# Eight input loads of a period: four pairs at neighbouring steps, or a step for each load, and a fourth result buffer

## The chip, the core and the metric

The kernel runs on one core of a Trainium2 chip. The metric is the time of one execution on the device in microseconds (us). The core has five engines that each work through a list of their own in order: TensorE (PE, matmuls, with the weight loads shown as PEld), VectorE (DVE), ScalarE (ACT), GpSimd (POOL) and SyncE (SP). Sixteen DMA engines move data; in this kernel SP issues the transfers of one queue and POOL those of another.

## The reference, cut to what matters

```python
# x: 8 x 3008 x 256, filt_r and filt_i: 1505 x 256
X = np.fft.rfft(x, axis=1)
y = np.fft.irfft(X * (filt_r + 1j * filt_i), n=3008, axis=1)
h = y.reshape(24064, 256) @ moe_w_in                     # 256 -> 2048
g = np.maximum(h, 0.0) + moe_alpha * np.minimum(h, 0.0)
out = g @ moe_w_out                                      # 2048 -> 256
```

## The kernel before, in words

The work has two halves that run side by side. The Fourier half takes one batch (3008 rows) at a time through four stages of small matmuls: piece_a (first DFT, reads a tile `xs` of x), piece_b (second DFT and product with the filter), piece_c (inverse of the second), piece_d (inverse of the first, written to `yT`). Between the stages the data goes out to device memory and comes back turned: `a_dram` between piece_a and piece_b, `v_dram` between piece_c and piece_d (`load_z`, L266). The product with a complex filter needs an exchange of the two halves of the partitions: after DVE has made `uu` and `ww`, POOL issues two adding transfers `uu<-ww` (L236), and piece_c reads `uu`.

The second half is the pair of dense layers, in 48 blocks of 512 (or 384) rows. A block has 16 steps; step s = 16n + j belongs to block n. In each step `up(j)` puts two matmuls of the first layer on PE (L495); after each second step ACT evicts (L503) and DVE applies the slope (L506, L507). The second layer of a block runs 16 steps behind, interleaved with the next block. In 21 of the blocks (`FAST`: 8, 10, 12 up to 42 by twos, then 43 to 45) it is done with seven products in place of eight, by `seven()`, whose 112 matmuls are on L554. Those need sums of quarters of the block, made by `sums()` at the steps of `SUMS`: DVE makes `ss`, and POOL issues adding transfers, one for each half h: `gtb<-gtb` (L519, at steps 16n+10 and 16n+17, read by the sixth product, matmuls 81 to 96) and `gtb<-ss` (L521, at 16n+20 and 16n+21, read by the seventh, matmuls 97 to 112). Below, "the first half" and "the second half" of a block's `gtb<-ss` are these two.

All the Fourier pieces are put into this stream by hand: `put(step, fn)` files a call under a step, and the loop over steps issues what stands there, so the list of steps is the order in which each engine gets its instructions. Nothing waits for the step itself: an instruction whose data is ready runs as soon as its engine has come to it. Batch b has its origin at p = 96(b-1), six blocks a batch; from batch 4 on all batches use the same lists of steps (STEPS_A, STEPS_B and so on), shifted by 96.

The loads of x are what the change touches. A batch's x comes in four tiles `xs` (index c), each filled by two transfers from POOL (L168, one a half of the partitions, 188 KB in float16, cast on the way from float32). There are four `xs` buffers, so the load of (b+1, c) must wait until piece_a of (b, c) has read its tile; piece_a of batch b stands at p-84 to p-43, and that of batch b+1 at p+12 to p+53. For batches 4 to 7 (b = 3 to 6) the pairs of loads stand at p-8, p-4, p and p+4:

```python
put(STEPS_X[b - 1][c] if b < 3 else p - 8 + 4 * c,
    lambda b=b, c=c: xc.update({(b + 1, c): load_x(b + 1, c)}))
```

The results go out through tiles `osb` (pool `p_osb`, three buffers): ACT or DVE fills one (L537, L565 to L572, L474), SP stores it (L464), and a buffer is free again once its stores have landed.

## Time and profile before

| what | value |
|---|---|
| median of 3 runs | 785.37 us (785.03, 785.37, 786.56) |
| the profiled execution | 783.02 us, of which the span is 780.6 us |
| PE busy | 759.1 us (97% of the span) |
| DVE, ACT, POOL busy | 687.2, 605.3, 277.3 us |
| granted TensorE clock | 1.000 |
| `uu<-ww` on POOL (L236) | 168 transfers of 64 KB, 3.2 us from issue to landing (median) |
| `gtb<-gtb` (L519), `gtb<-ss` (L521) | 42 each of 256 KB, 4.2 and 6.1 us |
| `xs<-in_x_dram` (L168) | 64 of 188 KB, 7.0 us |

The profile is of one execution. A line of the groups names the source line, the engine, what is written and what is read; "idle before" is the time that the engine stood still in front of such instructions, with what ended it. "DMA share" in a table of stretches is the mean busy share of the sixteen DMA engines; transfers that begin near its end make it read a little over 1. Spans on POOL are rough: its transfer instructions overlap, and what counts there is when one starts and when its data has landed.

### The profile page before, as it was taken

How to read it: one execution, taken by the hardware profiler on the slowest of the kernel's cores; microseconds unless marked ns; L12 is line 12 of the kernel's file. 1: busy time of each engine (PE TensorE's matmuls, PEld its weight loads, DVE VectorE, ACT ScalarE, POOL GpSimd, SP SyncE). 2: the span in 40 equal slices, each digit the busy share in tenths (PEclk: the TensorE clock that was granted, in tenths of full speed). 3: DMA queues.
4: the chain of work that ended last, by engine and by line, in shares of the span. 5: the costliest groups of instructions: out<-in, count | busy, mean ns of one | idle time of the engine just before them, and what ended most of it. 6: DMA issues, size and time to landing. Idle time of an engine off the chain costs nothing. (4 is left out here: it accounts for less than half of the span.)

```text
span 780.6 us, 18307 instructions
## 1 busy us (share of the span) xinstructions
PE 759.1 (97%) x6952; PEld 540.0 (69%) x6952; DVE 687.2 (88%) x1501; ACT 605.3 (78%) x902; POOL 277.3 (36%) x367
## 2 busy tenths in 40 slices
PE   7899999999999999999999999999999999999998
PEld 6756667666667767676676766767667777777666
DVE  3788996899999899899898989889899999889994
ACT  3787778788778887788877887788878777787763
POOL 7830651245244351553334423434323434102210
PEclk9999999999999999999999999999999999999999
DMA  9996868667988679975888769886797555735642
GB/s 185 193 198 177 154 123 208 177 135 148 202 193 175 148 145 194 236 148 125 169 213 176 138 135 200 188 173 129 160 201 175 112 113 95 180 84 112 121 96 68
DMA packets 115184, 122.93 MB, mean 157 GB/s; under 512 B 12873, under 2 KB 94553, under 8 KB 115097
## 3 DMA queue, kind: packets, MB, share of 16 engines
q0 software_dynamic: 34960, 52.19, 41.0%
q1 hardware_dynamic: 79992, 69.52, 33.4%
q8 instruction: 54, 0.88, 0.5%
q14 instruction: 34, 0.27, 0.1%
q10 hardware_dynamic: 144, 0.07, 0.0%
HBM read 56.06 MB, written 46.66 MB: 132 GB/s over the span
## 5 line engine op out<-in xcount | busy, mean ns | idle before, releaser
L503 ACT ACTIVATE gtb<-hps 128x1024 f16<-128x1024 f32 (+1 forms) x384 | 386.4, 1006 | 106.9 <-PE hps L495 104.3
L495 PE MATMUL hps<-yT,win_s 128*128 128x512 f16 (+1 forms) x1536 | 449.3, 375 | 0.0
L506 DVE TENSOR_SCALAR m<-gtb,alm_s 128x512 f16<-128x512 f16 (+1 forms) x768 | 235.1, 348 | 52.3 <-ACT gtb L503 50.2
L507 DVE TENSOR_TENSOR gtb<-gtb,m 128x1024 f16<-128x1024 f16 (+1 forms) x384 | 261.5, 681 | 17.2
L532 PE MATMUL op<-wout_s,gtb 128*128 128x256 f16 x1600 | 243.3, 272 | 0.0
L532 PEld LDWEIGHTS <-gtb 128*128 128x128 f16 x1600 | 156.0, 98 | 105.1
L236 POOL DMA_DIRECT2D uu<-ww x168 | 141.7, 1041 | 242.7 <-DVE uu L234 131.2
L495 PEld LDWEIGHTS <-win_s 128*128 128x128 f16 x1536 | 136.6, 98 | 25.7 <-issue 2.6
L554 PEld LDWEIGHTS <-gtb 128*128 128x128 f16 x1680 | 114.4, 98 | 57.4 <-DMA gtb<-ss 5.0
L519 POOL DMA_DIRECT2D gtb<-gtb x42 | 41.5, 987 | 197.8 <-DVE ss L515 75.5
L554 PE MATMUL op<-wout_s,gtb 128*128 128x128 f16 x1008 | 85.8, 219 | 4.1 <-DMA gtb<-ss 3.6
L280 ACT ACTIVATE asb<-psF 96x512 f16<-96x512 f32 x112 | 65.4, 595 | 11.5 <-PE psF L210 10.8
L280 ACT ACTIVATE yT<-psF 128x376 f16<-128x376 f32 x120 | 57.3, 490 | 11.0 <-PE psF L273 10.4
L554 PEld LDWEIGHTS <-ss 128*128 128x128 f16 x672 | 47.1, 98 | 23.3
L554 PE MATMUL op<-tw_s,gtb 128*128 128x128 f16 x672 | 58.2, 219 | 0.1
L554 PE MATMUL op<-tw_s,ss 128*128 128x128 f16 x672 | 58.0, 219 | 0.0
L233 DVE TENSOR_TENSOR ww<-psF,filts_s 128x512 f16<-128x512 f32 x84 | 57.4, 683 | 0.0
L234 DVE TENSOR_TENSOR uu<-psF,filt_s 128x512 f16<-128x512 f32 x84 | 57.1, 679 | 0.0
L280 ACT ACTIVATE v<-psF 128x512 f16<-128x512 f32 x84 | 49.9, 599 | 9.1 <-PE psF L248 8.3
L168 POOL DMA_DIRECT2D xs<-in_x_dram x64 | 43.2, 1054 | 20.9 <-PE psF L210 13.5
L521 POOL DMA_DIRECT2D gtb<-ss x42 | 45.7, 1290 | 3.2 <-PE op L554 0.9
L210 PE MATMUL psF<-xs,wf_s 94*96 94x512 f16 x112 | 41.2, 381 | 1.8 <-DVE yT L283 0.5
(85 smaller groups left out, 518.2 us busy)
## 6 DMA issues: line engine op xcount, KB each, us to landing
out_dram<-osb SPq DMA_DIRECT2D x127, 128.0 KB
xs<-in_x_dram POOLq DMA_DIRECT2D x64, 188.0 KB, 7.0
a_dram<-asb SPq DMA_DIRECT2D x28, 384.0 KB
uu<-ww POOLq DMA_DIRECT2D x168, 64.0 KB, 3.2
v_dram<-v SPq DMA_DIRECT2D x112, 96.0 KB
zt<-v_dram SPq DMA_DIRECT2D x28, 384.0 KB
gtb<-gtb POOLq DMA_DIRECT2D x42, 256.0 KB, 4.2
gtb<-ss POOLq DMA_DIRECT2D x42, 256.0 KB, 6.1
```

Of the source, the lines that this page charges most:

```text
L168: nc.gpsimd.dma_start(out=xs[h * N1 : h * N1 + N1], in_=xrow(b, h, c))
L233: nc.vector.tensor_mul(ww, px, filts_s[:, 2 * kp : 2 * kp + 2])
L234: nc.vector.tensor_mul(uu, px, filt_s[:, 2 * kp : 2 * kp + 2])
L236: nc.gpsimd.dma_start(out=uu[o : o + 64], in_=ww[64 - o : 128 - o], accum_op=OP.add)
L280: nc.scalar.activation(o, i, AF.Copy)
L495: nc.tensor.matmul(self.hps[:, j % 2, 0:tn], win_s[:, kt, j * 128 : (j + 1) * 128], yT[:, kt, self.t0 : self.t0 + tn], start=(kt == 0), st ...
L503: nc.scalar.activation(g, hs, AF.Copy)
L506: nc.vector.tensor_scalar(ms[:, i], g[:, i], 0.0, a, OP.min, OP.mult)
L507: nc.vector.tensor_add(g, g, ms)
L521: nc.gpsimd.dma_start(out=a12, in_=z2, accum_op=OP.add)
L532: nc.tensor.matmul(op[:, si % 2], self.pair(k // 2)[:, k % 2, 128 * si : 128 * si + 128], wout_s[:, k], start=(k == 0), stop=(k == 15))
L554: nc.tensor.matmul(acc[:, 128 * i : 128 * i + 128], x[:, k, 128 * i : 128 * i + 128], b[:, k], start=first and k + i == 0, stop=k == 7, sk ...
```

## The change

Each of the eight loads for batches 4 to 7 gets a step of its own, from a new list; the pair that belongs to tile c is at places 2c and 2c+1. The loads of batches 0 to 3 stay where they were. `p_osb` gets a fourth buffer, and the small tile `al16`, used once at the start, is taken from that pool in place of a place of its own.

```diff
+STEPS_Q = (-28, -18, -8, -3, 1, 9, 15, 23)
...
-    p_osb = ctx.enter_context(tc.tile_pool(name="p_osb", bufs=3))
+    p_osb = ctx.enter_context(tc.tile_pool(name="p_osb", bufs=4))
...
-    al16 = konst.tile([16, 128], FP32, name="al16")
+    al16 = p_osb.tile([128, 2, D], FP32, name="osb")[0:16, 0, 0:128]
...
-    def load_x(b, c):
-        xs = p_x.tile([2 * N1, 8 * D], FP16, name="xs")
-        for h in range(2):
-            nc.gpsimd.dma_start(out=xs[h * N1 : h * N1 + N1], in_=xrow(b, h, c))
-        return xs
+    def load_x(b, c, halves=(0, 1)):
+        if 0 in halves:
+            xc[(b, c)] = p_x.tile([2 * N1, 8 * D], FP16, name="xs")
+        for h in halves:
+            nc.gpsimd.dma_start(out=xc[(b, c)][h * N1 : h * N1 + N1], in_=xrow(b, h, c))
...
             for c in range(4):
-                put(STEPS_X[b - 1][c] if b < 3 else p - 8 + 4 * c,
-                    lambda b=b, c=c: xc.update({(b + 1, c): load_x(b + 1, c)}))
+                if b < 3:
+                    put(STEPS_X[b - 1][c], load_x, b + 1, c)
+                else:
+                    for h in range(2):
+                        put(p + STEPS_Q[2 * c + h], load_x, b + 1, c, (h,))
```

On PE, DVE, ACT and SP the order of instructions is the same before and after. On POOL it moves only the 32 loads of batches 4 to 7. With the block that begins at p-32 called the first of a period (n = 10, 16, 22 and 28), POOL's list there changes from the first row to the second:

```
before: uu x4 | L519, uu x2, L519, uu x2, L521 x2, xs x8      | uu x4, L519, uu x2, L519, L521 x2, uu x10
after:  uu x4, xs | L519, uu x2, xs, L519, uu x2, L521 x2, xs x3 | uu x4, xs, L519, uu x2, xs, L519, L521 x2, uu x2, xs, uu x8
```

(So it stands for n = 22 and 28. At n = 16 two `uu` stand in front of the first load instead of four; n = 10 has no `uu` between its transfers, since batch 3 has steps of its own.)

More of the change, by code (lines that the diff above doesn't have):

```diff
@@ L356 @@
     nc.sync.dma_start(out=wfx_s, in_=wfx_d.ap())
-    xc = {(0, c): load_x(0, c) for c in range(4)}
+    xc = {}
+    for c in range(4):
+        load_x(0, c)
     f0 = First()
@@ L434 @@
     for c in range(4):
-        xc[(1, c)] = load_x(1, c)
+        load_x(1, c)
     for q in range(2):
```

## The prediction

> **What bounds the kernel now.** I read the page first, then the waits of PE, then POOL's instructions in order of time around those waits, then the DMA share by stretches.

> ```profile
> PE 759.1 (97%) x6952; PEld 540.0 (69%) x6952; DVE 687.2 (88%) x1501; ACT 605.3 (78%) x902; POOL 277.3 (36%) x367
> ```

> PE is the bound, and the clock is 1.00 throughout. The change takes no matmul away and leaves PE's order alone, so it can only add or remove time in which PE stands still. The waits of PE and of its weight loads from 190 us on (the fast blocks begin there) say how much there is; columns are total us, times, longest:

> ```profile
> PE op L554 <- DMA gtb<-ss: 3.6, 5, 1.2
> PE psF L248 <- DMA uu<-ww: 1.1, 2, 0.9
> ...
> PEld L554 <- DMA gtb<-ss: 5.0, 6, 1.4
> PEld L248 <- DMA uu<-ww: 1.6, 2, 1.1
> ```

> A weight load and its matmul wait together, so the larger figure counts: 5.0 us for `gtb<-ss`, 1.6 for `uu<-ww`. By L521's own rows in narrow windows, three of these waits fall into n = 16 (0.9 us at 320.5), n = 22 (1.4 at 415.3) and n = 28 (1.0 at 509.1): 3.3 us in the blocks whose loads of x are moved. Those are the blocks where the eight loads stand right behind `gtb<-ss`; n = 34 has the same place in its period and no loads, since there is no batch 8. POOL in n = 28, then in n = 34 (start, us, what, idle before):

> ```profile
> 500.18 0.98 POOL L519 DMA_DIRECT2D gtb<-gtb  x1 [3.52 <-DVE ss L515]
> 501.38 1.66 POOL L236 DMA_DIRECT2D uu<-ww  x2 [0.22 <-issue]
> 502.44 2.54 POOL L521 DMA_DIRECT2D gtb<-ss  x2
> 503.62 5.27 POOL L168 DMA_DIRECT2D xs<-in_x_dram  x7
> ```

> ```profile
> 590.64 1.01 POOL L519 DMA_DIRECT2D gtb<-gtb  x1 [3.52 <-PE op L554]
> 591.85 1.66 POOL L236 DMA_DIRECT2D uu<-ww  x2 [0.19 <-PE hps L495]
> 593.87 1.77 POOL L521 DMA_DIRECT2D gtb<-ss  x2 [0.37 <-PE op L554]
> ```

> and L521's two transfers from issue to landing in n = 28, then in n = 34:

> ```profile
> DMA to landing us min/median/max: 4.5/5.8/7.0
> ```

> ```profile
> DMA to landing us min/median/max: 4.1/4.6/5.0
> ```

> n = 34 makes it in time, with 1.8 us to spare (landing 599.49, first read 601.31); n = 28 does not. That gap of 2.0 us in the second half's landing is what the change aims at, whatever its cause. The DMA engines around it (last columns: clock, DMA share, GB/s):

> ```profile
> 397.00:401.00 4.00, 4.00 (x30) 2.77 (x29) 3.90 (x10) 2.44 (x3) 2.34 (x3) 1.00 0.62 119
> 401.00:405.00 4.00, 4.00 (x42) 2.81 (x40) 3.82 (x8) 3.04 (x4) 0.21 (x1) 1.00 0.98 222
> 405.00:409.00 4.00, 4.00 (x52) 3.00 (x50) 3.93 (x10) 2.95 (x6) 3.16 (x6) 1.00 1.07 291
> ...
> 497.00:501.00 4.00, 4.00 (x50) 3.26 (x49) 3.86 (x9) 2.53 (x5) 0.82 (x1) 1.00 1.05 267
> 501.00:505.00 4.00, 4.00 (x59) 3.37 (x57) 3.90 (x12) 3.24 (x7) 3.78 (x8) 1.00 0.97 202
> ```

> They are full from about 401 and 497 us, well before `gtb<-ss` is issued (407.5 and 502.4): the three `zt` loads of SP and the stores of results run there.

> **The change, part by part.**

> *What a load costs where it stands.* On POOL a load takes about 0.53 us of issue (seven begin within 3.6 us). On the DMA engines, in the cluster with nothing of POOL's between, seven loads landed from 511.56 to 517.64 us: 6.08/6 = 1.01 us of all sixteen engines each, if they are full.

> *Two loads move ahead of the first block's transfers.* Nothing waits for a step, so the load of p-28 runs as soon as POOL has issued the `uu` before it; POOL then stands idle for 12.5 to 13.0 us until L519 of the first half. Cost nothing: that idle time hides it, and the half it precedes has 9.7 to 11.1 us to spare. The load of p-18 is issued right behind the next pair of `uu` (about 308.7, 400.6 and 496.1 us) and before L519 of the second half, which waits 3.8, 4.6 and 3.5 us for DVE and PE: no delay on POOL. On the DMA engines it is another matter. It begins to move about 2.3 us after issue (so the first of the cluster at 227.75 did), which is 311, 403 and 498 us, when the engines are full or about to be, and everything behind it in POOL's queue comes later by up to 1.01 us: L519 of the second half, then `gtb<-ss`, on which PE already waits. What the load finds free shortens that: by packet records about half an engine share at 310, 0.2 at 402 to 406, and 0.3 at 503 to 504. So the delay lies between 0.4 and 1.0 us at n = 16, 0.8 and 1.0 at n = 22, 0.7 and 1.0 at n = 28. I take 0.7, 0.9 and 0.8: **+2.4 us**. At n = 10 the same load is issued near 212 us, and the engines have free time until 219: nothing.

> *Five fewer loads behind `gtb<-ss`.* Three still follow at once (p-8, p-3, p+1), because POOL does not wait for their steps. Behind in a queue that is served in order they should cost the transfer ahead nothing; the 2.0 us between n = 28 and n = 34 say otherwise. But n = 34 also issued its `gtb<-ss` 1.0 us later behind its L519 (3.2 against 2.3), so fewer transfers stood in front. I count nothing for the five, since three loads are enough to fill the engines for the 3 us in question. The bound on the other side is the whole of the three waits, -3.3 us.

> [...]

> *Loads in the second block of a period* (n = 12, 18, 24, 30): p+9 ahead of the first half's L519 (11 to 13 us to spare), p+15 ahead of the second's, p+23 behind `gtb<-ss`. The second half of `gtb<-ss` lands 1.45, 2.80, 2.08 and 2.90 us before it is read. One load ahead takes 1.01: no wait. If the one behind cost the 2.0 us above too, n = 12, 24, 18 and 30 would lose 1.6, 0.9, 0.2 and 0.1: between 0 and +2.8; I take 0, as for the five.

> *`uu<-ww`.* The wait of 1.6 us near 486 us comes from `uu` issued at 477 to 478 that took about 8.9 us, beside SP's turn of `a_dram`. The load of p-28 comes right behind these. Between -1.6 (timing shifts) and +1; I take 0.

> *Arrival of x.* Tile 0 gains: it now lands 8.3 to 10.2 us before piece_a and comes 8 to 11 us earlier. The last load comes 20 to 25 us later, out of 34 to 39 us to spare. No wait; tiles 1 and 2 have 25 to 33 us and move by less. The buffers' readers (piece_a up to p-43) are done before p-28.

> *Fourth result buffer.* The three buffers were nearly short where the DMA engines are full: ACT stood 0.4 us before the result of n = 28 (L568) for a store to land, and PE did not wait there. A fourth removes that and would cover stores made later by the loads. On the path: nothing. `al16` is read once before the first result; nothing.

> **Sum.** +2.4 us. The profiled execution took 783.02 us (span 780.6 and 2.4 around it); it would take 785.4, a span of 783.0. The median of the runs stands 2.35 above that execution, so the forecast is 785.37 + 2.4 = **787.8 us**.

> **Rivals.**

> *Faster: the number of loads behind counts.* For it: n = 34. If the three waits vanish, 785.37 - 3.3 = 782.1 us; if the 2.0 us shrink with the number from eight to three, each block gains 1.25 and loses 0.8, 785.37 - 3 x 0.45 = 784.0. It decides from the point where the loads behind cost more than the load ahead. Against: L519 and `gtb<-ss` were already queued into full engines, and three loads follow as closely as before. Chance 0.33, most of it below 783.8.

> *No change: the load ahead is paid by others.* If the engines alternate between POOL's and SP's queues, the load of p-18 takes its time from the stores of results, which nobody waits for with four buffers. Then `gtb<-ss` lands as it did: 785.4 us. Chance 0.2.

> *Slower still: the second blocks wait too.* The +2.8 above on top of +2.4: 790.6 us. For it: only 1.45 and 2.08 us to spare at n = 12 and 24. Chance 0.08, within slower.

> *The change does not do what it says:* for three of the eight loads it does not, since a step is only a place in POOL's list; this is in the forecast already.

> **Numbers.** About 0.2% (1.6 us) is what a measurement of this kernel can tell from no change. Slower (above 786.9): 0.39 for the forecast and 0.08 for the last rival, 0.47 together. Same: 0.20. Faster (below 783.8): 0.33. The slower cases' own range is 787.0 to 790.6. Both signs hold much of the chance, so the range reaches from the faster rival's end, 782.0, to 789.8, just short of the slower rival's.

> **What would show it.** Right: in the profile after, L521's longest landing at 9.5 us in n = 22 (8.7 now) and 7.7 in n = 28 (7.0 now), and PEld's wait for `gtb<-ss` from 190 us at 7 us or more, in the same three blocks. Wrong: that wait at 2 us or less (the number of loads counted), or unchanged with the stores later. A new wait of L554 at n = 12 or 24 would be the last rival; one of piece_a (L210) for `xs` would refute the margins.

## The result, and the profile after

The changed kernel took 790.99 us (median of 8 runs, 785.44 to 792.95), the kernel before 784.81 us in the same comparison (8 runs, 781.39 to 786.93). The ratio is 1.0077, with a 95% interval of 1.0051 to 1.0103: slower by some 6 us. The side was forecast; the size was not (787.8 us, range 782.0 to 789.8). The profiled execution took 790.13 us with a span of 788.3 us, 7.7 us more than the span before.

The page after, first line of the busy times:

```profile
PE 760.2 (96%) x6952; PEld 540.5 (69%) x6952; DVE 687.5 (87%) x1501; ACT 605.3 (77%) x902; POOL 278.3 (35%) x367
```

The same matmuls, 1.1 us more of busy time, and the rest of the 7.7 us of span is PE standing still. The waits of PE and of its weight loads from 190 us on (total us, times, longest); all lines are three further down than before, so L524 is `gtb<-ss`, L522 `gtb<-gtb`, L557 the products, L274 piece_d, L249 piece_c, L170 the loads of x:

```profile
PE op L557 <- DMA gtb<-ss: 4.4, 5, 1.6
PE psF L274 <- DMA zt<-v_dram: 2.3, 1, 2.3
PE psF L249 <- DMA uu<-ww: 1.8, 1, 1.8
PE op L557 <- DMA gtb<-gtb: 1.4, 1, 1.4
...
PEld L557 <- DMA gtb<-ss: 5.3, 5, 1.8
PEld L274 <- DMA zt<-v_dram: 2.4, 1, 2.4
PEld L249 <- DMA uu<-ww: 2.0, 1, 2.0
PEld L557 <- DMA gtb<-gtb: 1.6, 1, 1.6
```

The wait on `gtb<-ss` hardly grew (5.0 us before). What is new is that piece_d waits 2.4 us for `zt`, once (at 319.5 us, in n = 16), that the sixth product waits 1.6 us for `gtb<-gtb` (n = 10), and that `uu<-ww` grew by 0.4. Together these lines give 11.3 us; `gtb<-ss`, `uu<-ww` and `gtb<-gtb` gave 6.9 before.

PE's order is the same, so the two traces can be set side by side matmul by matmul: the time that PE stood still between matmuls at each place, and by how much the matmuls behind the place then run later than before.

| place | stood still before, us | after, us | later by, us |
|---|---|---|---|
| up to 190 us | 9.2 | 11.0 | 1.1 |
| n = 10 | 0.9 | 2.0 | 1.2 |
| n = 16 | 1.2 | 2.7 | 3.2, of which 1.6 are lost at half clock |
| n = 22 | 1.2 | 2.2 | 1.2 |
| `uu<-ww` near 486 to 492 | 1.1 | 1.8 | 0.5 |
| n = 28 | 0.8 | 1.6 | 0.7 |
| n = 43 | 0.5 | 0.2 | -0.2 |

The first row and the last lie outside the moved loads; in the second profile of the same kernel the first 190 us are 0.1 us shorter than before, so the first row is not the change's. That profile (span 784.0 us) also divides the loss otherwise: of the places of the moved loads, n = 22 gains 1.4 us there and n = 28 loses 2.0. So one profile is weak evidence for one place, and several are compared below. The two measures of the table differ by up to 0.7 us (first row).

The half clock is in the table of stretches (last columns: granted clock, DMA share, GB/s):

```profile
316.00:319.50 3.50, 3.50 (x47) 2.85 (x45) 3.40 (x11) 2.81 (x6) 3.28 (x7) 1.00 0.81 134
319.50:322.90 3.40, 1.15 (x19) 0.84 (x16) 2.37 (x7) 0.79 (x3) 2.24 (x4) 1.00 0.99 262
322.90:326.30 3.40, 3.40 (x29) 2.71 (x27) 1.11 (x3) 2.45 (x5) 0.00 (x0) 0.50 1.10 238
326.30:330.00 3.70, 3.24 (x42) 2.41 (x40) 2.23 (x6) 2.46 (x6) 0.00 (x0) 1.00 1.06 223
```

PE is busy for 1.15 of 3.40 us, and in the next 3.41 us it is granted half its clock. A stretch of instructions there took 4.23 us; in a second profile of the same kernel, where the clock stayed at 1.00, it took 2.61. So the wait of 2.4 us cost 4.0 here.

POOL in n = 28 after (start, us, what, idle before), and the times from issue to landing of its two `gtb<-ss` there, then of those of n = 22 and n = 16:

```profile
502.10 1.65 POOL L237 DMA_DIRECT2D uu<-ww  x2 [1.56 <-PE hps L498]
503.18 1.12 POOL L170 DMA_DIRECT2D xs<-in_x_dram  x1
507.29 0.98 POOL L522 DMA_DIRECT2D gtb<-gtb  x1 [2.99 <-DVE ss L518]
508.49 1.65 POOL L237 DMA_DIRECT2D uu<-ww  x2 [0.22 <-issue]
509.55 2.51 POOL L524 DMA_DIRECT2D gtb<-ss  x2
510.73 2.90 POOL L170 DMA_DIRECT2D xs<-in_x_dram  x3
```

```profile
DMA to landing us min/median/max: 5.5/6.6/7.8
...
DMA to landing us min/median/max: 7.0/8.2/9.3
...
DMA to landing us min/median/max: 9.0/9.6/10.1
```

The second half now lands 7.8 us after issue at n = 28 (7.0 before), 9.3 at n = 22 (8.7) and 10.1 at n = 16 (6.7). At n = 16 the matmuls that read it came later still, since piece_d in front of them waited for `zt`.

Where `zt` was lost is on SP. Its list from the last eight stores of results before n = 16 to the loads of `zt`, before and then after:

```profile
298.23 6.99 SPq L464 DMA_DIRECT2D out_dram<-osb  x8
305.27 2.86 SPq L257 DMA_DIRECT2D v_dram<-v  x4
310.29 1.25 SPq L266 DMA_DIRECT2D zt<-v_dram  x3
```

```profile
301.29 8.97 SPq L467 DMA_DIRECT2D out_dram<-osb  x8
310.32 2.33 SPq L258 DMA_DIRECT2D v_dram<-v  x4
316.80 1.52 SPq L267 DMA_DIRECT2D zt<-v_dram  x3
```

and what SP's queue waited for there (from 294 us in both), before and then after:

```profile
SPq L266 <- DMA v_dram<-v: 2.0, 1, 2.0
SPq L464 <- DMA at<-a_dram: 1.1, 2, 0.9
```

```profile
SPq L267 <- DMA v_dram<-v: 4.0, 1, 4.0
SPq L467 <- DMA at<-a_dram: 2.8, 2, 1.6
```

In both traces SP's 479 transfers name eight semaphores in turn: 470 of the last 471 name the one that the transfer eight places before named, and 429 wait for the one that they name. Among the stores of results are those that follow an `at<-a_dram` by eight places. In front of the store eight places behind the last `at<-a_dram`, SP went on at 301.51 us before and 306.27 after, 0.02 and 0.01 us after the last signal that this `at<-a_dram` had landed. Behind these stores in SP's order stand those of `v_dram`, for which `zt` waits (the 2.0 and 4.0 us above). The load of p-28, issued at 293.72 us right behind `uu<-ww`, lands 10.8 us later, so it is in the DMA engines at the same time as the `at<-a_dram` of 291.56 us and later; the last of these four took 8.9 us from issue to landing before and 11.7 after. From the first `at<-a_dram` of the turn to the first load of `zt` it took 20.8 us before and 25.2 after. Some 3.0 us of that are lost up to the last four stores of `v_dram`, and 1.5 behind them, where SP waits 4.0 us in place of 2.0 for these stores; the load of p-18, issued at 310.98 us, stands beside them.

### The profile page after: what moved, and what is told of

Its sections match the earlier page's. It is cut to its first block, busy times and chain, and to the rows that moved or that the text cites. A ratio compares the mean times of both kernels' runs of the same rounds, so it can differ in the third digit from the quotient of the medians.

```text
span 788.3 us, 18315 instructions
## 1 busy us (share of the span) xinstructions
PE 760.2 (96%) x6952; PEld 540.5 (69%) x6952; DVE 687.5 (87%) x1501; ACT 605.3 (77%) x902; POOL 278.3 (35%) x367
## 4 chain that ended last, share of the span: by engine, by line
PE 77%; DMA 9%; DVE 7%; issue 3%; ACT 2%; POOL 2%; SPq 0%; DVEq 0%; POOLq 0%; ACTq 0%
PE hps L498 34%; PE op L535 19%; PE op L557 13%; DMA gtb<-ss 3%; PE psF L211 3%; PE psF L274 2%; PE psF L249 2%; PE psF L231 2%; DVE m L509 2%; DMA uu<-ww 2%; DVE gtb L510 2%; DMA zt<-v_dram 1%; ACT gtb L506 1%; DMA twf_s<-c_twf 1%; DVE ww L234 1%
## 5 line engine op out<-in xcount | busy, mean ns | idle before, releaser
L510 DVE TENSOR_TENSOR gtb<-gtb,m 128x1024 f16<-128x1024 f16 (+1 forms) x384 | 261.6, 681 | 17.2
L557 PEld LDWEIGHTS <-gtb 128*128 128x128 f16 x1680 | 115.0, 98 | 59.7 <-DMA gtb<-ss 5.3
L522 POOL DMA_DIRECT2D gtb<-gtb x42 | 43.0, 1024 | 187.4 <-DVE ss L518 72.1
L557 PE MATMUL op<-wout_s,gtb 128*128 128x128 f16 x1008 | 85.8, 219 | 4.9 <-DMA gtb<-ss 4.4
L281 ACT ACTIVATE asb<-psF 96x512 f16<-96x512 f32 x112 | 65.4, 595 | 11.5 <-PE psF L211 11.3
L557 PEld LDWEIGHTS <-ss 128*128 128x128 f16 x672 | 47.2, 98 | 23.5 <-issue 0.3
L170 POOL DMA_DIRECT2D xs<-in_x_dram x64 | 56.6, 1054 | 15.9 <-PE psF L211 14.2
L557 PE MATMUL op<-tw_s,gtb 128*128 128x128 f16 x672 | 58.9, 221 | 1.4 <-DMA gtb<-gtb 1.4
L557 PE MATMUL op<-tw_s,ss 128*128 128x128 f16 x672 | 58.2, 219 | 0.0
L524 POOL DMA_DIRECT2D gtb<-ss x42 | 45.0, 1252 | 3.2 <-PE op L557 1.0
L274 PE MATMUL psF<-wi_s,zt 96*128 96x94 f16 x504 | 39.8, 206 | 4.3 <-DMA zt<-v_dram 2.9
```

Of the source, the lines that this page charges most:

```text
L170: nc.gpsimd.dma_start(out=xc[(b, c)][h * N1 : h * N1 + N1], in_=xrow(b, h, c))
L274: nc.tensor.matmul(ps[:, m], self.zt[g][:, 4 * mh + m, dh * 128 : dh * 128 + 128], wi3_s, start=True, stop=True)
L281: nc.scalar.activation(o, i, AF.Copy)
L510: nc.vector.tensor_add(g, g, ms)
L557: nc.tensor.matmul(acc[:, 128 * i : 128 * i + 128], x[:, k, 128 * i : 128 * i + 128], b[:, k], start=first and k + i == 0, stop=k == 7, sk ...
```

## The experiments

The theory is that the two loads put ahead of the transfers cost the time: the one of p-18 as forecast, the one of p-28 by way of SP. The rivals are that the loads left behind `gtb<-ss` matter (fewer is faster, or the second blocks of a period suffer), and that the fourth buffer does something. The edits of `STEPS_Q` are to the changed kernel, in the order tile 0 to 3, two halves each. Ratios are to the kernel before run beside them, 5 rounds each, with the 95% interval.

**One part alone: four buffers.** The kernel before, with the fourth buffer and its `al16` only.

```diff
-    p_osb = ctx.enter_context(tc.tile_pool(name="p_osb", bufs=3))
+    p_osb = ctx.enter_context(tc.tile_pool(name="p_osb", bufs=4))
```

> The kernel before with the fourth result buffer alone (and the alpha tile taken from that pool); the loads of x stay in pairs at p-8 to p+4. Theory A (the moved loads cost the time): ratio to before 1.000, within 0.998 to 1.002. Rival B (a fourth buffer lets stores run later and crowds the transfers of the next blocks): 1.003 or more, and the waits of piece_d for zt and of the fast blocks for gtb<-ss grow as in the changed kernel.

Measured: 0.998 (0.9954 to 1.0005), 782.86 us.

**One part undone: three buffers, the loads moved.**

```diff
-    p_osb = ctx.enter_context(tc.tile_pool(name="p_osb", bufs=4))
+    p_osb = ctx.enter_context(tc.tile_pool(name="p_osb", bufs=3))
```

> The changed kernel with three result buffers: the new steps alone. Theory A: 1.006 to 1.010, like the whole change. If the fourth buffer hid stores that the loads make late, more than the whole change, 1.009 to 1.013, with waits of ACT for out_dram<-osb. Rival B: 1.002 or less.

Measured: 1.0104 (1.0065 to 1.0142), 790.59 us. Here PE had waits for an eviction by ACT that the changed kernel lacks, 1.5 us near 415 and 1.1 us near 510 us: ACT itself stood 2.0 and 1.6 us in front of a result buffer whose stores had not landed. So the moved loads make the stores late as well, and the fourth buffer hides that. It is worth something near 2 us beside the moved loads, with an interval that includes nothing.

**One load ahead, or none.**

```diff
-STEPS_Q = (-28, -18, -8, -3, 1, 9, 15, 23)
+STEPS_Q = (-28, -8, -8, -3, 1, 9, 15, 23)
```

> The changed kernel with the load of p-18 put back to p-8: of the two loads ahead of the first block's transfers only that of p-28 is left, and four follow gtb<-ss. Theory A1 (the load of p-28 falls on SP's turn of a_dram; SP's list slips, and the zt loads come 2 to 6 us late): most of the loss stays, 1.004 to 1.008, with the zt loads of n = 16 issued 3 us or more later than before. Theory A2 (the forecast's step: the load of p-18 stands in the queue ahead of gtb<-ss): 1.000 to 1.002.

```diff
+STEPS_Q = (-18, -8, -8, -3, 1, 9, 15, 23)
```

> The changed kernel with the load of p-28 moved to p-18 and that of p-18 to p-8: one load stands ahead of L522's second half, none behind the uu of p-42 and p-41. Theory A1: 1.000 to 1.003, with the zt loads of n = 16 issued at the same step as before (273). Theory A2: most of the loss stays, 1.003 to 1.006, with the gtb<-ss waits of n = 16, 22 and 28 at 5 us together.

```diff
+STEPS_Q = (-8, -8, -8, -3, 1, 9, 15, 23)
```

> The changed kernel with both early loads put back: tile 0's two loads at p-8, so five loads follow gtb<-ss in the first block of a period and the other three stay at p+9, p+15 and p+23. If the two early loads are the whole loss (theory A), 0.997 to 1.000, as the fourth buffer alone (0.998). If the loads at p+9 to p+23, in the second block, cost something of their own (rival C), 1.002 or more, with a wait of the seventh product for gtb<-ss at n = 12, 18, 24 or 30 of 1 us or more.

Measured: p-28 alone 1.0025 (1.0005 to 1.0046), 786.78 us; p-18 alone 1.0015 (0.9993 to 1.0037), 785.94 us; none ahead 0.9991 (0.9965 to 1.0018), 783.5 us. Without the early loads the loss is gone, with five loads behind `gtb<-ss` in place of eight and three spread over the second blocks. PE's weight loads wait there as they did before:

```profile
PEld L557 <- DMA gtb<-ss: 5.2, 7, 1.1
PEld L249 <- DMA uu<-ww: 1.4, 2, 1.2
```

SP's list with p-28 alone, same place as above:

```profile
300.90 7.87 SPq L467 DMA_DIRECT2D out_dram<-osb  x8
308.83 2.10 SPq L258 DMA_DIRECT2D v_dram<-v  x4
313.78 2.30 SPq L267 DMA_DIRECT2D zt<-v_dram  x3
```

The time from the turn's first `at<-a_dram` to the first `zt` before n = 16, 22 and 28, in the profiles of all kernels that have eight loads a batch, three or more behind `gtb<-ss` and none at p-43:

| kernels | n = 16, us | n = 22 | n = 28 |
|---|---|---|---|
| no load at p-28: before, four buffers, none ahead, p-18 alone (two profiles), two at p-18 | 20.8 to 21.8 | 15.3 to 17.2 | 16.7 to 17.1 |
| one load at p-28: changed (two profiles), p-28 alone, three buffers | 23.3 to 25.2 | 17.6 to 19.5 | 17.8 to 18.0 |
| two loads at p-28 | 23.9 | 19.7 | 20.9 |

At all three places every kernel with the load is above every kernel without it, by 0.4 us at the least. The transfers of the turn themselves tell the same: the last of the four `at<-a_dram` takes 8.9 to 9.5, 7.9 to 8.4 and 9.0 to 9.4 us to land in the kernels of the first row, and 10.4 to 11.7, 9.1 to 10.0 and 10.2 to 10.4 us in those of the second. The load at p-18 alone does not move SP.

**Two loads at one place.** Both early loads at p-18, then both at p-28.

```diff
+STEPS_Q = (-18, -18, -8, -3, 1, 9, 15, 23)
```

> The changed kernel with both loads of tile 0 at p-18, none at p-28; three behind gtb<-ss as in the changed kernel. Theory A2 (what counts is the number of bytes ahead of gtb<-ss in POOL's queue): L522's second half and gtb<-ss of n = 16, 22 and 28 come another 1 us later than with one load there: 1.006 to 1.010. Theory A3 (it takes both places together: the load of p-28 delays SP's list, so that its zt loads meet the load of p-18): 1.002 to 1.005.

```diff
+STEPS_Q = (-28, -28, -8, -3, 1, 9, 15, 23)
```

> The changed kernel with both loads of tile 0 at p-28, none at p-18; three behind gtb<-ss as in the changed kernel. Theory A2: nothing ahead of gtb<-ss that has not long landed: 0.998 to 1.001. Theory A1 (SP's list is what slips): 1.005 to 1.010, with the zt loads of n = 16 issued 5 us or more later than before and piece_d waiting for them. Theory A3: 1.002 to 1.005.

Measured: two at p-18 1.0099 (1.0064 to 1.0134), 792.12 us; two at p-28 1.0056 (1.0033 to 1.0078), 788.76 us. Two directly ahead of `gtb<-gtb` and `gtb<-ss` are the dearer pair, by 0.0043, just clear of the two intervals.

**Loads behind.** None behind and two at p-28; none behind and none close ahead (two at p-43 instead); six behind with the same two at p-43.

```diff
+STEPS_Q = (-28, -28, 8, 8, 22, 22, 24, 24)
```

> The changed kernel with tile 0's two loads at p-28 and the other six at p+8 (two), p+22 (two) and p+24 (two): no load follows gtb<-ss in the first block, two run ahead, none at p-18. Rival D (loads behind gtb<-ss slow it, so taking all of them away gains): gtb<-ss lands 4 to 5.5 us after issue at n = 16, 22 and 28, and the ratio is 0.993 to 0.998. Theory A1 (loads behind SP's turn of a_dram make the zt loads late): zt loads of n = 16 are issued 3 us or more late, gtb<-ss lands no sooner than before, 1.002 to 1.008.

```diff
+STEPS_Q = (-43, -43, 7, 7, 23, 26, 28, 33)
```

> The changed kernel with the loads laid around the first block of a period: tile 0's two at p-43, behind gtb<-ss of the block before and ahead of SP's turn of a_dram (p-39); tile 1's two at p+7, tiles 2 and 3 at p+23, p+26, p+28 and p+33. None stands ahead of or behind gtb<-ss at n = 16, 22 and 28. Rival D (the loads behind slow gtb<-ss): it lands 4 to 5.5 us after issue there, as at n = 34, the three waits vanish, and the ratio is 0.994 to 0.998. Theory A (only loads ahead of it cost): it lands as in the kernel with none ahead (6.9 to 8.2 us for the second half), 0.998 to 1.002. If the loads at p-43 still meet SP's turn, the zt loads of n = 16 are issued late again and the ratio is 1.002 or more.

```diff
+STEPS_Q = (-43, -43, -4, -4, 0, 0, 4, 4)
```

> The changed kernel with tile 0's two loads at p-43 and the other six in pairs at p-4, p and p+4, all six behind gtb<-ss of the first block, as in the kernel before with eight. Rival D: gtb<-ss lands 1 to 2.5 us later at n = 22 and 28 than in the kernel with none behind, and the ratio is 0.002 to 0.004 higher than there. Theory A: it lands the same within 0.5 us, and the two ratios agree within 0.002.

Measured: 1.0183 (1.0146 to 1.022), 800.7 us (five runs; a sixth took 811.2 us); 1.0114 (1.0081 to 1.0148), 793.09 us; 1.0137 (1.0108 to 1.0166), 795.36 us. In the first, PE's weight loads wait 9.7 us for `uu<-ww`, in five places (1.6 us before, 3.4 at the most elsewhere). The last two differ only in where the other six loads stand. Their times from issue to landing of `gtb<-ss` at n = 16, with none behind and then with six:

```profile
DMA to landing us min/median/max: 8.8/9.2/9.6
```

```profile
DMA to landing us min/median/max: 8.6/9.0/9.3
```

At n = 22 the second half landed after 8.0 us (none) and 6.7 (six), at n = 28 after 7.9 and 9.1. Loads behind don't slow it in any regular way, and with none behind it is about as slow as in the changed kernel (9.6, 8.0 and 7.9 us against 10.1, 9.3 and 7.8). So the rival finds no support here; both kernels carry the loads at p-43, so it was not tried by itself. The loads at p-43 meet the turn as well: from `at<-a_dram` to `zt` it takes 24.0 us with none behind, 23.1 with six.

**The changed kernel again**, and then its two early loads cut to an eighth in turn. An eighth is the first of the eight rows that each partition takes; the other seven eighths stand at p-8.

> The changed kernel once more, on the chip of the others of this call: 1.005 to 1.010 under every theory. It is the reference for the kernel with the cut load, and a second look at where its waits fall.

```diff
+                        if c == h == 0:
+                            put(p - 28, load_x, b + 1, c, (h,), 0, D)
+                            put(p - 8, load_x, b + 1, c, (h,), D, 8 * D)
```

> The changed kernel with the load of p-28 cut in two transfers: one eighth of its columns at p-28, the other seven eighths at p-8; the load of p-18 stays. If it is the bytes at p-28 that cost (A1), as the kernel with the load of p-18 alone: 1.000 to 1.003. If any transfer in that place does (its turn in POOL's list, its semaphore), as the whole change: 1.006 to 1.010.

Measured: again 1.0069 (1.0045 to 1.0093), 789.38 us, which is the 1.0077 of before; with an eighth at p-28 1.0062 (1.0035 to 1.0088), 788.87 us. The second was to come down to the time of p-18 alone and did not, though SP was back (21.7 us from `at<-a_dram` to `zt`). Either any transfer at p-28 costs, whatever its bytes, or the time of p-18 alone is higher than it seemed. Four kernels on one chip:

> The kernel with the load of p-18 alone ahead (the other at p-8), once more, beside the three kernels that follow. Two theories of what an early load costs. Bytes: the early load costs by the 188 KB that it puts in front of SP's turns and of gtb<-ss. Place: any transfer of POOL at that place costs, however small, because the later transfers of POOL move up by one. Both expect here what this kernel gave before, a ratio of 1.0015 (1.000 to 1.0035), about 786 us.

```diff
+STEPS_Q = (-8, -8, -8, -3, 1, 9, 15, 23)
+                        if c == h == 0:
+                            put(p - 28, load_x, b + 1, c, (h,), 0, D)
+                            put(p - 8, load_x, b + 1, c, (h,), D, 8 * D)
```

> No load ahead but one eighth of a load at p-28 (one eighth of tile 0's first half, its other seven eighths at p-8, where the second half stands too). Bytes: as with none ahead, a ratio of 0.999 (0.997 to 1.0015), 783.5 us, zt loads of n = 16 at step 272 to 273. Place: 1.003 or more, since the same small transfer beside the load of p-18 went with 1.0062.

```diff
+                        if c == 0 and h == 1:
+                            put(p - 18, load_x, b + 1, c, (h,), 0, D)
+                            put(p - 8, load_x, b + 1, c, (h,), D, 8 * D)
```

> The changed kernel with the load of p-18 cut to one eighth there, the other seven eighths at p-8; the load of p-28 stays whole. Bytes: what the load of p-28 alone gave, a ratio of 1.0025 (1.0005 to 1.0045), 787 us, with the second half of gtb<-ss landing 1 us sooner than in the changed kernel at n = 16 (9 instead of 10.1 us from issue). Place: as the changed kernel, 1.007 (1.005 to 1.009), 790 us.

> One eighth of a load at p-28 and the whole load at p-18, once more, now beside the load of p-18 alone on the same chip. Bytes: the two agree within 0.002, near 1.0015, and the 1.0062 of before was a difference between chips. Place: 1.006 again, at least 0.003 above the load of p-18 alone.

Measured: p-18 alone 1.0002 (0.9982 to 1.0022), 784.72 us; the eighth at p-28 alone 1.0027 (1.0005 to 1.0049), 786.79 us; p-28 whole and an eighth at p-18 1.009 (1.0058 to 1.0121), 790.81 us; an eighth at p-28 and p-18 whole 1.0063 (1.004 to 1.0085), 788.87 us. So it looked as if the place costs, whatever the bytes. But all these kernels have nine transfers a batch where the others have eight. Two more put the ninth elsewhere:

```diff
+STEPS_Q = (-18, -8, -8, -3, 1, 9, 15, 23)
+                        if c == 0 and h == 1:
+                            put(p - 8, load_x, b + 1, c, (h,), 0, D)
+                            put(p - 8, load_x, b + 1, c, (h,), D, 8 * D)
```

> The load of p-18 whole (tile 0's first half), and the second half of tile 0 in two transfers, one eighth and seven eighths, both at p-8, behind gtb<-ss. Nine transfers a batch, as in the kernels with an eighth at p-28 and the load of p-18, which gave 1.0062 and 1.0063. Place: the small transfer at p-28 is what costs there, so here the ratio is that of the load of p-18 alone, 1.001 (0.999 to 1.003), 785.5 us. Number: it is the ninth transfer, wherever it stands, so here 1.006 again (1.004 to 1.008), 789 us.

```diff
-                            put(p - 8, load_x, b + 1, c, (h,), 0, D)
+                            put(p - 18, load_x, b + 1, c, (h,), 0, D)
```

> As the kernel with both parts of the second half at p-8, but its eighth stands at p-18, right behind the whole load there, ahead of gtb<-gtb of the second half. Place at p-28: no loss beyond that of the load of p-18 alone, since the eighth is 0.2 us of the DMA engines by the packets of the kernel with it alone: 1.001 (0.999 to 1.003). Any transfer ahead of gtb<-gtb and gtb<-ss: 1.006 (1.004 to 1.008), as with the eighth at p-28. SP's order at the steps of the load of p-18 alone in both (its eighth transfer after the last at<-a_dram at step 263 before n = 16).

Measured: the eighth at p-8 1.0062 (1.0036 to 1.0089), 788.35 us; at p-18 1.0043 (1.0019 to 1.0067), 786.53 us. Place falls. With p-18 whole, a load split in two gives 1.0062, 1.0063 and 1.0062, 1.0043, with its small part at p-28 (twice), p-8 and p-18. An eighth at p-28 costs nothing beyond the split itself, which agrees with the theory of the bytes. The split costs 0.003 to 0.005 beside the 1.0009 of p-18 alone (mean of two), as the expectation by number has it. In the profile of the split at p-8 SP is where it was with p-18 alone at the first two places (20.9 and 16.8 us); at n = 28 it takes 18.2 us in place of 16.7 and 16.8, and so it is in all six profiles with nine transfers (18.2 to 20.4 us), with and without a transfer at p-28. The wait for `gtb<-ss` is twice that of p-18 alone too; the split kernel, then p-18 alone (second profile):

```profile
PEld L557 <- DMA gtb<-ss: 8.3, 5, 2.5
```

```profile
PEld L557 <- DMA gtb<-ss: 4.3, 5, 1.3
```

Why a ninth transfer does that stays open. POOL's transfers, too, name eight semaphores in turn (all of the last 345 of 353 in both profiles the one named eight places before), and a ninth shifts that turn by one in each batch; no run tries this.

## Why the prediction was right or wrong

**The load of p-18: the delay came, the wait did not, except at n = 16.** It was priced at 2.4 us. p-18 alone, the mean of its two comparisons less none ahead, is 1.0009 - 0.9991 = 0.0018, or 1.4 us; the intervals allow about 2.4 us to either side, so the time decides neither for 2.4 us nor for nothing. The profiles say more. The transfer right behind the load, `gtb<-gtb` of the second half, did land later: 7.4 and 8.7 us from issue at n = 16, 6.6 and 6.7 at n = 22, 5.7 and 5.8 at n = 28, against 6.4, 3.8 and 4.7 with none ahead. But PE's weight loads did not wait longer for `gtb<-ss` at two of the three places (us, in the stretch of each block):

| kernels | n = 16 | n = 22 | n = 28 |
|---|---|---|---|
| before | 0.9 | 1.4 | 1.0 |
| four buffers | 1.1 | 1.3 | 1.0 |
| none ahead | 1.1 | 0.9 | 0.9 |
| p-28 alone | 2.4 | 0.7 | 0.9 |
| p-18 alone (two profiles) | 1.7, 1.3 | none, none | 0.9, 1.0 |
| both, the changed kernel (two profiles) | none (2.4 for `zt`), 2.3 | 2.5, none | 1.8, 3.1 |
| two at p-18 | 1.5 | 2.4 | 2.2 |
| two at p-28 | 3.4 | 3.5 | 3.6 |

The forecast was 0.7, 0.9 and 0.8 us more. Alone, the load adds 0.2 and 0.6 us at n = 16 beside none ahead, and 1.7 and 0.8 us of wait for `gtb<-gtb` in front of it; it takes the wait away at n = 22 and does nothing at n = 28. At n = 28 it needs two early loads: with one or none the wait is 0.9 to 1.0 us in six profiles, with two it is 1.8 to 3.6 in four. (With three buffers PE was held up by ACT there instead.) Why n = 22 gains no run shows. At n = 10, where nothing was expected, 1.2 us were lost in the first profile, and `gtb<-gtb` (7.0 us to landing before, 8.2 after) was late itself.

**The load of p-28: wrong, and this is the step that failed.** "Cost nothing: that idle time hides it" looked at POOL alone, and at the half of `gtb<-gtb` behind the load. Alone it costs 1.0025 - 0.9991 = 0.0034, or 2.7 us (intervals: about as much to either side, so the time by itself hardly tells it from nothing), and the traces show it where the prediction did not look: SP's turn of `a_dram`, in the DMA engines at that moment, lands later; a store eight places behind holds SP; `zt` slips, in the four profiles with one load there by 2.5 to 4.4 us at n = 16, 0.4 to 2.3 at n = 22 and 0.7 to 0.9 at n = 28; and `zt` then moves together with `gtb<-gtb` and `gtb<-ss`. The prediction named that turn for `uu<-ww`, and took 0 there too (0.4 us more in the first profile, 0.3 less in the second), but did not ask what stands behind the turn in SP's list. In the 7 us that begin 1.44 us behind the turn's first `at<-a_dram` before n = 16, the packets of POOL's queue took 37.3% of the sixteen engines' time before and 47.3% after, those of SP's queue 75.4% and 66.1%; the turn lost 4.4 us. That the slip comes from this load, and that the `at<-a_dram` beside it land later, is shown by the table and the times below it. That it costs by the bytes it moves is likely and not shown: with an eighth of it the turn took 20.7, 21.7 and 23.1 us at n = 16, two of the three within the range without the load.

**The sum.** The two alone make 0.0018 + 0.0034 = 0.0052; together they cost 1.0073 (mean of two comparisons) less 0.9991 = 0.0082, or 6.4 us. The rest of 0.003 is within the intervals. Three things speak for a sum that is more than its terms, which the prediction did not allow for. One is the row of n = 28 above. One is SP: from the last four stores of `v_dram` to `zt` before n = 16 it took 5.0 us before and with p-28 alone, 4.9 and 5.7 with p-18 alone, and 6.1 to 6.5 in the three profiles with both, where the late stores meet the load of p-18. The third is the clock. Over 8 runs of the changed kernel the granted clock averages 0.9976, in the 19 runs of the kernel before beside the second comparison 0.9990. Each 0.001 is 0.79 us of the span, so by this estimate the clock makes at most 1.1 of the 6 us. The prediction priced waits at their own length.

**No cost or gain for fewer loads behind: right as far as it was tried.** None ahead and five behind is 0.9991, no gain from three fewer; none behind against six, with two at p-43, is 1.0114 against 1.0137, within the intervals. POOL's 353 transfers land in the order of their issue, without an exception in either of the profiles before and after. So the faster rival (782.1 to 784.0 us, 0.33) loses its evidence: n = 34 differs from n = 28 by more than the loads. That the loads pay by stores (the rival of no change) is half seen: both queues had a part of the engines at once (at 308 to 309 us in the profile before, POOL's packets took 45.7% of the engines' time and SP's 52.4%), and with three buffers the stores do come late enough for ACT to wait, but at n = 16 `gtb<-ss` came late as well (9.8 us for the second half, 6.7 before).

**Second blocks: right.** No new wait of L557 at n = 12 or n = 24, in either profile of the changed kernel; n = 30 had one of 0.8 us in the second. The slower rival's number (790.6 us) is near the result by another mechanism.

**Arrival of x: right.** L211 (piece_a) has no wait for `xs` in the changed kernel. **The fourth buffer: nothing on the path** in the kernel before (0.998, an interval that includes 1), but not idle beside the moved loads.

**What was to show it.** The longest landing at n = 22 and 28 was to be 9.5 and 7.7 us; it was 9.3 and 7.8 in the first profile. That is luck: in the second it was 6.5 and 9.1, and with p-18 alone, the load it was worked out for, 6.4 to 6.5 and 6.9 to 7.0. PE's wait for `gtb<-ss` was to be 7 us or more in the same three blocks; it was 5.3 in the first profile, since piece_d had waited in its place, and 8.3 in the second, where n = 22 had none. The base makes the miss larger: the median before was 784.81 us in this comparison, not 785.37, so the kernel lost 6.2 us where 2.4 were forecast.

## What to carry to other kernels

A transfer moved into an idle stretch of its own queue was not free here, where another queue was in the DMA engines: SP's turn before n = 16 took 25.2 us in place of 20.8. So follow that queue's list to what it issues next, and to where it must wait for the transfer that was delayed. Price a move of a load by the time at which it really moves, not by its step. Try the parts of a change alone before their prices are added: here two early loads together made a wait of 1.8 and 3.1 us at n = 28, where each by itself left it at 0.9 to 1.0. And keep the number of transfers the same in such trials: here a split in two cost 0.003 to 0.005, as much as the moves under study. A PE wait cost more than its length here: the one that left PE busy for 1.15 of 3.40 us cost its 2.4 us and 1.6 us more at half clock.

## What the runs showed of the hardware

**Mean clock and time.** On the whole the mean clock of the runs falls as the time grows: 0.9985 with none ahead (783.5 us), 0.9976 changed (791.0), 0.9947 with loads at p-43 and none behind (793.1), 0.9930 with none behind and two at p-28 (800.7). In the last, 0.0055 less than none ahead is, by the estimate of 0.79 us for each 0.001, at most 4.3 of the 17.2 us.
